# An attention and dense kernel whose instruction order comes from a planner: changed load times, engines for weight casts, and places for the q and k transposes

## The chip, the core and the metric

The kernel runs on one core of one Trainium2 chip. The core has five engines with an instruction queue each: TensorE (PE in the profile; its weight loads are shown as PEld), VectorE (DVE), ScalarE (ACT), GpSimd (POOL) and SyncE (SP), which here starts all DMA transfers. Each engine takes its instructions in the order in which the program gives them; between engines there are semaphores. The metric is the device time of one execution in microseconds. The numbers of a profile come from one profiled execution.

## What is computed

The input is q, k and v of 8 batches x 8 heads x 576 tokens x 64 channels in float32, and two weight matrices of 512 x 2048 and 2048 x 512. Cut to what matters, the reference is

```python
# attention, per batch and head
q_d, k_d, v_d = means of q, k, v over 4 tokens each      # 144 tokens
out_up    = repeat(softmax(q_d k_d^T / 8) v_d, 4)
out_local = softmax(q k^T / 8 where |i - j| < 4) v       # a band of 7
x = (out_up + out_local) as 4608 tokens x 512 channels
# dense part
h = x @ w_in                                             # 4608 x 2048
out = (h - tanh(h)) @ w_out                              # 4608 x 512
```

## The kernel before

**Attention.** Two heads of one batch make a pair: 32 pairs p, four to a batch. Two pairs make a group: 16 groups n. For a group, `load_qk(n)` brings q and k (four transfers of 288 KB) into a staging buffer `qkn`, `reorder(n, i)` casts them to bfloat16 into `qr` (i = 0 is q, i = 1 is k), and `turn(n, i)` transposes them with nine TensorE matmuls into a PSUM bank, copies the bank to `qk` and forms the sums over four tokens in two steps (`half`, then `qkd`). `qr`, `qk` and `qkd` have two buffers, one for even and one for odd groups; `half` has one. `load_v(p)` brings the v windows of a pair into one of six buffers `vst`, and `prep_v(p)` casts them to `vw`. The sums of v come from TensorE for groups 0 to 6 (`pool_v`), and from GpSimd (`load_v4`, `sum_v`, one buffer) from group 7 on.

`attention(p)` is a generator in steps: the scores of the band (`s1`, line 508, and the last tile with the pooled scores, `s2`, lines 508 and 527), three exponentials on ScalarE (lines 547, 562, 565), two multiplications with the mask on VectorE (551, 569; pairs 0 to 3 have a bias on TensorE instead, line 502), the products with v (`outs`, 580 and 586), the reciprocal `r` (595) and the scaled result `ln` (597) on VectorE. Up to pair 11 `ln` is transposed back on TensorE (631 to 635), copied (`od`, 638) and added into `xT` (640); from pair 12 on a DMA transpose does it (605) and VectorE adds (616). The scores use the banks `ps_ts`, the products with v `ps_ox`, and pairs 0 and 2 a second pair of banks, which later becomes the four banks `ps_hy` of the dense part.

**Dense part.** It has nine blocks of 512 tokens. `mm1(kb, fc)` multiplies `xT` with `w_in_sb` (line 663, four matmuls), ScalarE takes the tanh (672) and VectorE subtracts into `gT` (675). `mm2(kb, i)` multiplies `gT` with `w_out_sb` (691), ScalarE copies (702) and SyncE stores (705). From block 2 on, `mm1` of a block alternates with `mm2` of the one before. A block straddles two batches in most cases, and block 7 reaches into the last batch.

**Weights.** `load_w` brings a quarter of `w_in` or `w_out` (1 MB) in float32 into memory that is not yet in use (`gT`, late parts of `xT`), and four casts (line 397) write the bfloat16 weights. Each of them may go to one of the engines in `CAST`.

**The order.** No order is written out by hand. Every step is an `op` with an engine, a cost in nanoseconds, the buffers that it reads and writes, and a priority `pri`; `P.choice` is an op with several engines to choose from, each with a cost. `Program.order` is a list scheduler: it keeps a time at which each engine is free and each op is ready, and gives an engine that comes free the ready op with the lowest `pri`. The dense matmuls have pri 5000, so in the plan they fill what attention leaves. An op is ready when its inputs are written plus a lag by engine (`LAT`, 1800 ns for a DMA); for ops with a pri from 140 to 4999 `P.spare` adds 2500 ns behind a DMA and 1000 behind GpSimd. Transfers have planned costs: `T_QK` 760, `T_V` 800, `T_W` 2750 ns. The plan is made when the program is built; on the chip only its order remains. `idle` and `emit` find gaps of TensorE in the plan ahead of the first dense matmul, and `filler` puts matmuls on a constant there (line 869).

Where a group is reordered and turned is set in the main loop over p by program order (buffers make later readers and writers wait) and by pri (`20 * n - 12` and `20 * n`). The lists of the loop are

```python
inner = INNER.get(p, [p % 2] if p >= 2 * NP else [])    # ahead of pair p's last step
outer = OUTER.get(p, [])                                # behind it
```

so from pair 8 on, an even pair turns q of the next group and an odd pair its k. `load_qk`, `load_v` and `load_v4` of group n wait in SyncE's queue for the DMA transpose of pair 2n - 5.

Of the kernel before, what the change touches and what calls it, by code (L numbers as in the profile page):

```python
# [9 lines left out]
BF16 = mybir.dt.bfloat16  # L10
# [5 lines left out]
class Program:  # L16
# [10 lines left out]
    def __init__(self):  # L27
        self.ops = []
        self.alternatives = {}
        self.touch = []  # L30
        self.fresh = set()
        self.spare = (5000, {})
        self.last_write = {}
        self.readers = {}
# [27 lines left out]
    def order(self):  # L62
        n = len(self.ops)
# [15 lines left out]
        for _ in range(n):  # L79
# [11 lines left out]
            now, eng, i = best  # L91
# [9 lines left out]
            for u in users[i]:  # L101
                same = self.ops[u][0] == eng and eng != "DMA"
                lag = self.LAT[eng]
                if self.spare[0] <= self.ops[u][4] < 5000:
                    lag += self.spare[1].get(eng, 0)
                at[u] = max(at[u], end if same else end + lag)
                left[u] -= 1
                if left[u] == 0:
                    make_ready(u)
# [45 lines left out]
def kernel(  # L155
# [9 lines left out]
    nc = tc.nc  # L165
# [8 lines left out]
    A6 = 9  # L174
# [67 lines left out]
    P = Program()  # L242
    P.spare = (140, {"DMA": 2500, "POOL": 1000})
    op = P.op
# [50 lines left out]
    def load(ns, fn, keys, cost, pri, after=()):  # L295
        op("SP", ns, fn, reads=after, writes=list(keys) + ["queue", ("q", keys[0])],
           pri=pri)
        op("DMA", cost, None, reads=[("q", keys[0])], writes=keys, pri=pri)

    def slot_qk(n):  # L300
        return n % 2 if n >= GV else n % NQKN
# [30 lines left out]
    def load_qk(n):  # L332

        b, h0, s = n // 2, 4 * (n % 2), slot_qk(n)
        for i, src in enumerate((q, k)):
            for y in range(2):
# [7 lines left out]
                def issue(to=to, rows=rows):  # L344
                    nc.sync.dma_start(out=to, in_=rows)  # L345
                load(650, issue, [("qkn", s, i, y)], T_QK, -30,
                     [("fl", 2 * n - AHEAD)])

    def load_v(p):

        b, j, s = p // NP, p % NP, p % NVST
        t = vst[s]
# [24 lines left out]
    def load_w(src, dst, name, f, stage, keys):  # L377

        def issue():
# [4 lines left out]
            else:  # L384
# [4 lines left out]
                else:  # L389
                    nc.sync.dma_start(  # L390
                        out=stage.rearrange("p (c f) -> p c f", c=4),
                        in_=rows[:, 4 * f:4 * f + 4, :])
        load(600, issue, keys, T_W, -30)
        for c in range(4):
# [7 lines left out]
    def prep_v(p):  # L402
        s, w, jj = p % NVST, (p // 2) % NVW, p % 2
        P.choice([(eng, ns, lambda fn=fn: fn(  # L404
# [5 lines left out]
    def pool_v(hb):  # L410
# [6 lines left out]
        def mm():  # L417
# [7 lines left out]
           writes=[key], pri=pri)  # L425
        op("ACT", 300, lambda: A.copy(
            out=vd[w][:, :, :, 0:64],
# [18 lines left out]
    def turn(n, i):  # L446
# [5 lines left out]
        pri, cold = 20 * n, (1.5 if n < 1 else 1.0)  # L452
        b16 = ps.rearrange("p n c -> p (n c)").bitcast(BF16)[:, 0:A6 * 128]

        def tr():
            for a in range(A6):
                T.transpose(b16[:, 128 * a:128 * a + 128], qr[s][:, i, a, :], ident)  # L457
        P.fresh.add(len(P.ops))
        op("PE", 480 * cold, tr, reads=[("qr", s, i), "ident"], writes=ts, pri=pri)
        o = qk[s][:, :, KOFF * i:KOFF * i + 576]  # L460
# [249 lines left out]
    def dense(kb):  # L710
# [13 lines left out]
        for i in range(16):  # L724
            if kb < NBLK:
# [5 lines left out]
    XOUT, T_OUT, AHEAD = 12, 2000, 5  # L731
    MERGE, GV = 14, 7
    XADD = [("DVE", (800, 350), V)]
    ORDER, W_FIRST = "g0123", "0123g"
    INNER, OUTER = {4: [0], 5: [1]}, {3: [0, 1], 7: [0, 1]}
    T_QK, T_V, T_W, W_PRI, NEARLY = 760, 800, 2750, 33, NP
    CAST = [("POOL", 700, GP.tensor_copy), ("ACT", 520, A.copy)]
    CAST_V = [[("POOL", 720, GP.tensor_copy), ("ACT", 640, A.copy)],
              [("POOL", 790, GP.tensor_copy)]]
# [4 lines left out]
            [("ACT", 1125, A.copy)]]  # L744
    ADDERS = [[("DVE", 750, 440, V), ("POOL", 1190, 750, GP)],
              [("POOL", 1190, 880, GP)]]
# [89 lines left out]
    for p in range(NPAIR):  # L836
# [5 lines left out]
        if p >= 2:  # L842
            next(work[p])
        inner = INNER.get(p, [p % 2] if p >= 2 * NP else [])
        outer = OUTER.get(p, [])
        for i in inner if n + 1 < NGRP else []:
            reorder(n + 1, i)
            turn(n + 1, i)
        next(work[p], None)
        for i in outer:  # L850
            reorder(n + 1, i)
            turn(n + 1, i)
        if p % 2 == 1:
# [47 lines left out]
```

The softmax here doesn't subtract the row's maximum and nothing guards it: scores larger than these inputs give would overflow.

## Time and profile before

| | |
|---|---|
| median of 6 runs | 344.28 us (343.4 to 345.75) |
| profiled execution, its time | 343.4 us |
| its span in the profile | 341.7 us |
| mean granted TensorE clock | 0.985 |
| dense matmuls, L663 and L691 | 576 + 576, 292.9 us busy |
| largest on ScalarE | tanh, L672, 83.6 us in 144 |
| largest on VectorE | subtraction, L675, 95.6 us in 144 |
| largest on GpSimd | first half sum, L473, 34.3 us in 29 |
| DMA | 57.51 MB, mean 168 GB/s |

The page has six parts: busy time by engine; the span in 40 slices of 8.5 us, with a digit for the tenths busy; the DMA queues; the chain of waits that ended last; the costliest groups of instructions with the idle time of the engine before them and what ended it; and the DMA issues. Matmuls are pipelined, and the duration of one includes its way through the array, so that the time from one start to the next is the better measure of what it costs. In a timeline a row is: start, duration, engine, line, operation, operands, number of instructions, and in brackets the idle time of the engine before the row and its releaser. In a table of stages a row is: stretch and length, then busy time (instructions) of PE, PEld, DVE, ACT and POOL, then granted TensorE clock, DMA share and GB/s.

The chain that ended last runs over TensorE for 82% of the span, over DMA for 7% and over VectorE for 5%. The first dense matmul starts at 26.30 us, the last ends at 337.95.

### The profile page before, as it was taken

To read this page: it belongs to the slowest core of one execution; us is meant where nothing else is said; L and a number is where in the kernel's file an instruction comes from. 1 tells how busy PE (TensorE), PEld (TensorE's weight loads), DVE (VectorE), ACT (ScalarE), POOL (GpSimd) and SP (SyncE) were. 2 spreads that over 40 slices of the span, in tenths; PEclk is the share of its full clock that TensorE was granted. 3 is DMA by queue.
4 is the path that set the end of the run, shared out by engine and by line. 5 is a ranking of instruction groups with operands and counts; after the bars stand their busy time and mean duration, and the time that the engine had idled before them with its cause. 6 is when DMAs were issued, how large, how long until landed. Compare 5 with 4: busy or idle time off the path is not lost.

```text
span 341.7 us, 6832 instructions
## 1 busy us (share of the span) xinstructions
PE 325.2 (95%) x2616; PEld 168.4 (49%) x2616; DVE 216.1 (63%) x360; ACT 204.7 (60%) x342; POOL 151.0 (44%) x179
## 2 busy tenths in 40 slices
PE   5887999989999999999999999999999999999995
PEld 1563554645655555555555555554544444444442
DVE  4775785459987677777797668776776453343300
ACT  2685996559868665766576657665755244344411
POOL 8444847596694165939393818491300000000000
PEclk9698999999999999999999999999999999999999
DMA  6999999999802598689979579952222200100021
GB/s 209 263 389 295 280 361 322 267 296 290 220 2 59 155 248 215 187 210 193 238 162 245 157 197 214 237 155 58 59 58 60 58 31 33 61 31 33 31 88 66
DMA packets 84749, 57.51 MB, mean 168 GB/s; under 512 B 62638, under 2 KB 67822, under 8 KB 84718
## 3 DMA queue, kind: packets, MB, share of 16 engines
q1 hardware_dynamic: 84718, 57.09, 60.1%
q8 instruction: 20, 0.33, 0.4%
q14 instruction: 11, 0.09, 0.1%
HBM read 43.05 MB, written 9.44 MB: 154 GB/s over the span
## 4 chain that ended last, share of the span: by engine, by line
PE 82%; DMA 7%; DVE 5%; SPq 2%; ACT 1%; issue 1%; POOL 0%; DVEq 0%; ACTq 0%; POOLq 0%
PE ps_hy L663 34%; PE ps_hy L691 33%; PE ps_ts L457 3%; DMA vst<-in_v_dram 3%; PE ps_ts L508 3%; PE ps_ox L580 3%; DMA qkn<-in_q_dram 3%; PE ps_ox L586 2%; DVE ln L597 1%; DMA qkn<-in_k_dram 1%; SPq L369 1%; SPq L345 1%; DVE gT L675 1%; DVE qr L441 1%; PE ps_ox L457 1%
## 5 line engine op out<-in xcount | busy, mean ns | idle before, releaser
L663 PE MATMUL ps_hy<-xT,w_in_sb 128*128 128x512 bf16 x576 | 147.3, 382 | 3.4 <-DVE xT L640 2.7
L691 PE MATMUL ps_hy<-w_out_sb,gT 128*128 128x512 bf16 x576 | 145.6, 379 | 0.0
L672 ACT ACTIVATE uy<-ps_hy 128x512 f32<-128x512 f32 x144 | 83.6, 600 | 78.4 <-PE ps_hy L663 77.7
L675 DVE TENSOR_TENSOR gT<-ps_hy,uy 128x512 bf16<-128x512 f32 x144 | 95.6, 684 | 55.1 <-ACT uy L672 54.5
L663 PEld LDWEIGHTS <-w_in_sb 128*128 128x128 bf16 x576 | 53.7, 98 | 62.7 <-issue 5.9
L691 PEld LDWEIGHTS <-gT 128*128 128x128 bf16 x576 | 53.5, 98 | 59.5
L473 POOL TENSOR_TENSOR half<-qk 128x576 f32<-128x576 bf16 x29 | 34.3, 1182 | 58.3 <-ACT qk L463 57.2
L463 ACT COPY qk<-ps_ts 128x1152 bf16<-128x1152 bf16 x28 | 31.5, 1126 | 15.9 <-PE ps_ts L457 13.8
L702 ACT COPY uy<-ps_hy 128x512 f32<-128x512 f32 x36 | 21.2, 588 | 22.1 <-PE ps_hy L691 20.5
L547 ACT ACTIVATE E<-ps_ts 128x960 bf16<-128x960 f32 x30 | 29.2, 974 | 6.8 <-PE ps_ts L508 6.7
L597 DVE TENSOR_TENSOR ln<-ps_ox,r 128x896 bf16<-128x896 f32 x30 | 32.7, 1090 | 0.9
L551 DVE TENSOR_TENSOR E<-E,mask 128x960 bf16<-128x960 bf16 x28 | 22.2, 791 | 10.8 <-ACT E L547 10.5
L404 POOL CAST vw<-vst 128x640 bf16<-128x640 f32 x31 | 23.6, 774 | 10.7 <-DMA vst<-in_v_dram 8.4
L457 PEld LDWEIGHTS <-qr 128*128 128x128 bf16 x288 | 19.5, 102 | 12.6 <-DVE qr L441 5.7
L322 POOL TENSOR_TENSOR qkn<-qkn 128x512 f32<-128x512 f32 (+1 forms) x18 | 23.8, 1320 | 2.9 <-DMA qkn<-in_v_dram 2.1
L441 DVE CAST qr<-qkn 128x1152 bf16<-128x1152 f32 x18 | 15.3, 848 | 13.7 <-DMA qkn<-in_q_dram 10.6
L457 PE MATMUL ps_ts<-ident,qr 128*128 128x128 bf16 x252 | 19.1, 222 | 4.1 <-DVE qr L441 2.6
L478 POOL TENSOR_TENSOR qkd<-half 128x288 bf16<-128x288 f32 x30 | 21.7, 724 | 2.3 <-DVE half L473 1.3
L616 DVE TENSOR_TENSOR xT<-lnT 128x480 bf16<-128x480 bf16 (+1 forms) x40 | 22.0, 562 | 0.0
L441 POOL CAST qr<-qkn 128x1152 bf16<-128x1152 f32 x14 | 17.0, 1217 | 9.5 <-DMA qkn<-in_k_dram 7.7
L595 DVE RECIPROCAL r<-ps_ox 128x14 f32<-128x14 f32 x30 | 7.3, 243 | 20.0 <-PE ps_ox L586 18.1
L580 PE MATMUL ps_ox<-vw,E 128*128 128x65 bf16 x300 | 18.3, 194 | 1.2 <-DVE E L569 1.2
(87 smaller groups left out, 253.0 us busy)
## 6 DMA issues: line engine op xcount, KB each, us to landing
vst<-in_v_dram SPq DMA_DIRECT2D x62, 160.0 KB, 5.2
qkn<-in_q_dram SPq DMA_DIRECT2D x32, 288.0 KB, 3.4
qkn<-in_k_dram SPq DMA_DIRECT2D x32, 288.0 KB, 5.1
out_dram<-uy SPq DMA_DIRECT2D x36, 256.0 KB, 2.1
qkn<-in_v_dram SPq DMA_DIRECT2D x9, 512.0 KB, 4.9
gT<-in_moe_w_in_dram SPq DMA_DIRECT2D x4, 1024.0 KB, 10.1
xT<-in_moe_w_out_dram SPq DMA_DIRECT2D x8, 256.0 KB, 4.4
gT<-in_moe_w_out_dram SPq DMA_DIRECT2D x2, 1024.0 KB, 9.6
```

The costliest lines, as they stand in the source:

```text
L322: op("POOL", 1330, lambda t=t: GP.tensor_tensor(out=t[:, :, 0:2], in0=t[:, :, 0:2], in1=t[:, :, 2:4], op=ALU.add), writes=keys, pri=pri)
L441: P.choice([(eng, ns, lambda fn=fn: fn(out=dst, in_=srt)) for eng, ns, fn in REORDER[n >= 2][i]], reads=[("qkn", sn, i, x) for x in range(2)],
L457: T.transpose(b16[:, 128 * a:128 * a + 128], qr[s][:, i, a, :], ident)
L463: fn(out=o.rearrange("p y (g a) -> p y g a", a=A6), in_=b16.rearrange("p (a g y) -> p y g a", a=A6, y=2))
L473: eng.tensor_tensor(out=half, in0=four[:, :, :, 0:2], in1=four[:, :, :, 2:4], op=ALU.add)
L547: op("ACT", 980, lambda: A.activation(out=e1, in_=ps[:, :, 0:480], func=AF.Exp, scale=SCALE), reads=ts, writes=[("E", se, 0)], pri=pri)
L580: T.matmul(po[:, hh, 65 * t:65 * t + 65], E[se][:, c:c + 128], vw[w][:, 2 * jj + hh, t, :], start=True, stop=True)
L597: op("DVE", 1090, lambda: V.tensor_tensor(out=ln[sl].rearrange("p n (h d) -> p h n d", d=D), in0=blocks[:, :, :, 0:64], in1=r[s].unsqueeze ...
L663: T.matmul(ps_hy[slot], w_in_sb[:, dc, fc * 128:(fc + 1) * 128], xT[dc][:, kb * 512:kb * 512 + 512], start=(dc == 0), stop=(dc == N_DC - 1))
L672: op("ACT", 490, lambda: A.activation(out=u[us], in_=ps_hy[slot], func=AF.Tanh), reads=[("hy", slot)], writes=[("u", us)], pri=-1)
L675: op("DVE", 620, lambda: V.tensor_tensor(out=gT[g][:, fc, :], in0=ps_hy[slot], in1=u[us], op=ALU.subtract), reads=[("hy", slot), ("u", us) ...
L691: T.matmul(ps_hy[slot], gT[g][:, fc, ts * 128:ts * 128 + 128], w_out_sb[:, fc, :], start=(fc == 0), stop=(fc == N_FF - 1))
```

## The change

Nothing is computed otherwise. The change gives the planner other numbers and other program places, and the order on every engine comes out anew.

- `P.spare` becomes a function: behind a DMA 2500 ns from pri 140 on as before, and 1500 for pri 80 to 139, where there was nothing; behind GpSimd as before.
- Planned transfer costs: q and k 840 in place of 760, the k of group 0 1260; the first and second quarter of `w_in` 300 and 1400 more.
- The casts of the weights may go to VectorE too (planned at 400 ns). Planned costs on ScalarE and GpSimd change: weight casts, v casts, the copy of the pooled v (300 to 600), the half sums.
- `EARLY = 12`: up to pair 11 the lists are as before. Pair 12 turns q and k of group 7. From then on an odd pair p turns, behind its last step, q of the group after next (m = n + 2), and an even pair turns k of the next group.
- A branch of `turn` for groups from `FI` on transposes q and k by DMA into a `vst` buffer, and `slot_v` leaves two buffers free for it. `FI` is 99, there are 16 groups and 32 pairs.

```diff
-    P.spare = (140, {"DMA": 2500, "POOL": 1000})
+    def spare(pri, eng):
+        if eng == "DMA":
+            return 2500 if pri >= 140 else 1500 if pri >= 80 else 0
+        return 1000 if eng == "POOL" and pri >= 140 else 0
+    P.spare = spare
...
+    def slot_v(p):
+        return p % 4 if p >= 2 * FI else p % NVST
...
-                load(650, issue, [("qkn", s, i, y)], T_QK, -30,
+                load(650, issue, [("qkn", s, i, y)],
+                     T_QK + (500 if n == 0 and i == 1 else 80), -30,
                      [("fl", 2 * n - AHEAD)])
...
-        load(600, issue, keys, T_W, -30)
+        load(600, issue, keys, T_W + (W_LATE[f] if src is moe_w_in else 0), -30)
...
-        op("ACT", 300, lambda: A.copy(
+        op("ACT", 600, lambda: A.copy(
...
+        if n >= FI:
...
-        P.fresh.add(len(P.ops))
-        op("PE", 480 * cold, tr, reads=[("qr", s, i), "ident"], writes=ts, pri=pri)
+        if n < FI:
+            P.fresh.add(len(P.ops))
+            op("PE", 480 * cold, tr, reads=[("qr", s, i), "ident"], writes=ts, pri=pri)
...
+    FI, T_IN, EARLY = 99, 2600, 12
...
+    W_LATE = [300, 1400, 0, 0]
...
-    CAST = [("POOL", 700, GP.tensor_copy), ("ACT", 520, A.copy)]
-    CAST_V = [[("POOL", 720, GP.tensor_copy), ("ACT", 640, A.copy)],
+    CAST = [("POOL", 620, GP.tensor_copy), ("ACT", 620, A.copy),
+            ("DVE", 400, V.tensor_copy)]
+    CAST_V = [[("POOL", 790, GP.tensor_copy), ("ACT", 720, A.copy)],
...
-    ADDERS = [[("DVE", 750, 440, V), ("POOL", 1190, 750, GP)],
+    ADDERS = [[("DVE", 760, 440, V), ("POOL", 1190, 850, GP)],
...
-        inner = INNER.get(p, [p % 2] if p >= 2 * NP else [])
-        outer = OUTER.get(p, [])
+        inner = INNER.get(p, [] if p < 2 * NP else [p % 2] if p < EARLY else
+                          [0, 1] if p == EARLY else [1] if p % 2 == 0 else [])
+        m = n + 1 + (p > EARLY)
+        outer = OUTER.get(p, [0] if p > EARLY and p % 2 else [])
...
-        for i in outer:
-            reorder(n + 1, i)
-            turn(n + 1, i)
+        for i in outer if m < NGRP else []:
+            reorder(m, i)
+            turn(m, i)
```

The number and kind of instructions stay, but for seven more filler matmuls (10 become 17). Of the eight weight casts that go to VectorE, five are of `w_in`. The SyncE queue keeps the order of its loads.

## The prediction, made before the changed kernel was run

> **What bounds the kernel now.** I read the page's shares first, then the slices, then TensorE's timeline with its idle times, then the same stretches on VectorE and ScalarE, then busy times by stage.
>
> ```profile
> PE 325.2 (95%) x2616; PEld 168.4 (49%) x2616; DVE 216.1 (63%) x360; ACT 204.7 (60%) x342; POOL 151.0 (44%) x179
> ...
> PE   5887999989999999999999999999999999999995
> ...
> DMA  6999999999802598689979579952222200100021
> ```
>
> TensorE is the bound: 325.2 of 341.7 us. The 1152 dense matmuls stay, and in long runs they start every 0.216 us (8 in 1.73 us in the chain of waits), so they are 248.8 us that no order shortens. What an order can save is TensorE's idle time and slow clock. The idle time lies at the start, where DMA is full, and in four places later:
>
> ```profile
> 29.32 3.18 PE L663 MATMUL ps_hy<-xT,w_in_sb 128*128 128x512 bf16 x8 [1.20 <-DVE xT L640]
> 57.51 0.23 PE L631 MATMUL ps_ox<-ident,ln 128*128 128x128 bf16 x1 [0.61 <-DVE ln L597]
> 69.10 0.38 PE L508 MATMUL ps_ts<-qk 64*128 64x120 bf16 x8 [1.01 <-ACT qk L463]
> 77.19 0.20 PE L580 MATMUL ps_ox<-vw,E 128*128 128x65 bf16 x1 [1.22 <-DVE E L569]
> 273.20 3.46 PE L663 MATMUL ps_hy<-xT,w_in_sb 128*128 128x512 bf16 x14 [0.67 <-ACT uy L702]
> ```
>
> In brackets is the idle time before a row and who ended it: 0.61 + 1.01 + 1.22 = 2.84 us in the middle. At the end 0.67 understates it: the 8 matmuls that started at 270.63 should have handed over at 272.36, so 0.84 is lost, and the 14 take 3.46 where 14 x 0.216 and the last one's tail of 0.16 make 3.19, 0.27 more: 1.1 us. From 77 to 270 us nothing else stands still. Behind the middle stalls stands one pattern:
>
> ```profile
> 55.16 1.01 DVE L441 CAST qr<-qkn 128x1152 bf16<-128x1152 f32 x1 [2.35 <-DMA qkn<-in_q_dram]
> ...
> 68.04 1.12 DVE L441 CAST qr<-qkn 128x1152 bf16<-128x1152 f32 x1 [1.35 <-DMA qkn<-in_q_dram]
> ...
> 76.20 0.76 DVE L441 CAST qr<-qkn 128x1152 bf16<-128x1152 f32 x1 [3.37 <-DMA qkn<-in_q_dram]
> ```
>
> VectorE takes its instructions in order. The planner believed these q loads to be in earlier, and put the casts of groups 4, 6 and 7 ahead of work that TensorE waits for: r and ln of pair 5, ln of pair 7, the second mask (L569) of pair 8.
>
> **Middle stalls.** I compared the issue orders of the two kernels. In the new one the cast of group 4 stands behind ln of pair 5 and the first mask of pair 6, that of group 6 behind ln of pair 7, that of group 7 behind ln of pair 8. So the masks of pair 8 now stand behind group 6, which landed at 68.0, and no longer behind group 7, which landed at 76.2. That takes 0.61 and 1.22 away. The 1.01 at 69.10 is another chain: ScalarE's copy of group 4's k waited 2.02 us for GpSimd's half sum of q, which ran at 66.73 behind a cast that waited for group 5's k (63.84), a memset (0.95) and a v cast (0.73). In the new order the half sum stands ahead of all but the v casts that landed by 59.6. q is turned after 104 dense matmuls, not 110 (6 x 0.216 = 1.3 us earlier, about 61.8); its copy (1.12) ends about 63.5, the half sum (1.15) at 64.7, the copy of k at 66.0, and S1 of pair 8 falls due at about 66.8. Nothing is waited for. What is late next is group 7's q (76.2): behind it stand a subtraction and the mask of pair 9, due near 77, so the cover is thin; I keep 0.3 for it. Sum: -2.84 + 0.3 = -2.5.
>
> **End stall.** q of group g was turned in pair 2g-2 and k in pair 2g-1. From group 8 on, q is turned as pair 2g-3 ends, and k in pair 2g-2. The attention of the next group no longer waits for transpose, copy (1.12), half sum (1.18) and sum (0.72) of k within its last pair, so the planner packs pairs closer: from pair 12 to pair 31 there were 31 dense matmuls a pair (216 to 810), and there are 24 (230 to 680). Block 7 of the dense part, which starts at dense matmul 832, needs pair 31. Before, that was 22 matmuls behind; the planner split block 7 (2, then 8 of the second product, then 14) and the banks ran out at 273.2. Now pair 31 is 152 matmuls (33 us) ahead, and the order there is the even 8 and 8 seen later without a gap. -1.1.
>
> **Start.** The loads and their order are the same, so the landings are too. Three q/k casts go from VectorE to GpSimd (0.76 or 1.58 becomes about 1.15), two q/k copies from ScalarE to VectorE (1.12 becomes 1.36), one v cast from ScalarE to GpSimd, and five w_in casts come to VectorE. I follow the path to xT of pair 3, which starts the dense stream. k of group 0 is cast at 7.98 + 1.2 = 9.2, where VectorE was ready at 9.56. Its transpose, copy and sums then run as before within 0.3 us; q of group 1 is about 0.3 later, and the v copies (vd) follow both last exponentials of pair 1, which shifts outs of pair 0 from 17.8 to about 18.4-18.9. ln of pair 0 ends at 20.4 (was 19.98). The VectorE queue from there: two w_in casts, xT 0.75, ln of pairs 2 and 1, a cast, two xT, ln of pair 3 (1.09), then transposes and xT. The sum of the rows puts xT of pair 3 at 29.7, where it was 29.27: +0.4. Two prices in it are open.
>
> First the casts: VectorE shows no 512-column cast. From the 1152-column row (0.76) I estimate 0.37 each; but that form took 1.58 at 7.98, while GpSimd ran a half sum. The Trainium skill (GPSIMD Engine Reference, Specifications) says that both engines share the SBUF interfaces and contend when VectorE runs a two-port mode. It speaks against this part: a slab's casts now start on both engines as it lands. With the quiet row the three casts ahead of the last ln cost 1.1, with the disturbed one 2.3. Two would run beside GpSimd's two casts (1.2 us at 19.8), so I add 0.3 of the 1.2: start +0.7.
>
> Second the clock:
>
> ```profile
> 3.90:7.30 3.40, 1.62 (x13) 0.62 (x11) 0.78 (x1) 0.71 (x1) 3.33 (x8) 1.00 0.90 291
> 7.30:10.70 3.40, 1.09 (x10) 1.09 (x11) 2.33 (x2) 0.41 (x1) 2.41 (x3) 0.61 1.01 324
> ...
> 20.90:24.30 3.40, 2.73 (x69) 2.29 (x67) 2.63 (x5) 2.70 (x8) 1.21 (x4) 1.00 1.04 386
> 24.30:27.70 3.40, 1.47 (x12) 0.75 (x13) 3.19 (x5) 2.09 (x5) 1.74 (x4) 1.00 1.06 391
> 27.70:31.10 3.40, 2.20 (x12) 0.97 (x11) 1.22 (x2) 1.91 (x4) 1.18 (x2) 0.63 1.11 342
> ```
>
> The first figure after the length is TensorE's busy time, the third from the right its granted clock. The skill (TensorE: Matmul & The Clock Gate, What's actually happening) lets the clock fall to half after at least one idle window of about 3.4 us; by that, no gap here (1.5 us at most) costs clock, and the seven filler matmuls that are added gain nothing. The rows disagree: behind windows busy 1.62 and 1.47 of 3.40 the clock fell (0.61, 0.63), behind 2.73 it held. The new fillers (five for two) make the window from 3.9 about 1.95 busy. If that holds the clock, transposes and scores from 9 to 14 us run twice as fast and the path gains 0.9; if not, nothing. 1.95 is nearer to 1.62 than to 2.73, so I take nothing; -0.9 stays for the range.
>
> **The faster stretch.** A pair took (262.5 - 97.8)/19 = 8.7 us. With 24 for 31 dense matmuls it is 1.5 us shorter, 7.2. Per pair VectorE has ln 1.09, r 0.24, masks 0.79 + 0.47, xT 0.79 + 0.33, half a q cast 0.42 and three subtractions of 0.68: 6.2 of 7.2 (86%). The cover is there: from 80 to 100 us it was busy 18.7 of 20 and TensorE had no gap. GpSimd has 5.4 of 7.2, ScalarE about the same. DMA stood at 0.81 from 140 to 220; times 8.7/7.2 that is 0.98, full. A group's loads took 12.5 us from the first q to the pooled v4, of 14.4 that a group now lasts, and q is wanted about 13 us after its trigger. It fits without much room: +0.4 for small waits. TensorE's turns into 64-row scores (0.31 for 0.22 to the next start) grow by about three, +0.3 at most, within that.
>
> **Sum.** -2.5 - 1.1 + 0.7 + 0.4 = -2.5. The profiled execution took 343.4 (span 341.7, 1.7 around it), so 340.9 against it. It is also the fastest of the six shown, whose median is 0.9 above; I forecast the median of the new one at **341.8**.
>
> **Rivals.**
> - *The stalls move instead of going* (0.20). DMA is full to 77 us, and no load lands sooner; TensorE, with 1-2 us fewer dense matmuls done, would meet the next cast at 76.2. For it: no landing moves. Against it: the masks no longer stand behind that cast. Then only the end goes: 343.4 - 1.1 + 0.7 + 0.4 = 343.4; median 344.3, no change.
> - *Slower: the fuller loads hold up the pooled sums* (0.15). From group 9 on GpSimd puts all four v4 sums (4.3 us) between q's two sums, and k's follow. If v4 lands over 2 us later than 12.5 us after its q, GpSimd waits, k's sums slip by as much, and beyond some 5 us of slack TensorE waits at S1 of each next group. It decides from 0.5 us a group (seven groups, 3.5 us). At 1 us: 340.9 + 7 = 347.9; median 348.8. For it: DMA at 0.98. Against it: two margins, together 7 us.
> - *The start gains as well* (0.10, faster): clock held and quiet casts, -0.9 and -0.3: 340.6.
> - The branch with the DMA transpose never runs (FI = 99) and `slot_v` gives the old slot: that part does nothing.
>
> **Numbers.** The forecast has 0.55, the rivals 0.20, 0.15 and 0.10. A difference under 0.3% (1.0 us) can't be told from none. Faster: 0.55 + 0.10, plus 0.03 of the first rival: 0.68. Same: 0.15. Slower: 0.15 and 0.02 of the first: 0.17. Range 339.5 (all stalls gone, clock held, no new waits) to 345.2, which takes in the first rival and leaves out most of the second.
>
> **What would show it.** Right: no idle time over 0.3 us on TensorE from 50 to 100 us, none near 273, block 7 in even runs, VectorE near 86% until about 240 us and GpSimd done by then; the first 8 dense matmuls at 29.5-30.2. Wrong: waits of L508 for qkd or qk from 120 us on (second rival), L569 again behind a load, or a dense stream that starts past 31.

## The result, and the profile after

The changed kernel took 347.81 us in the median of 29 runs (343.81 to 351.72), the kernel before 344.82 us of 66 (343.04 to 348.88). The ratio is 1.0058 [1.0041, 1.0076]: **slower by 0.6%**, where 341.8 and "faster" were forecast, and outside the range of 339.5 to 345.2. All ratios here leave out the slow runs, those over 1.5% above the fastest of their kernel (11 of the changed kernel's 30 with the profiled one), which is why this one is below the quotient of the two medians, 1.0087. The profiled execution (351.08 us) is one of the longest of its kernel, for a reason given under the clock below.

The page of the changed kernel, in the lines that were shown of before, and the chain of work that ended last (shares of the span by engine):

```profile
PE 329.4 (94%) x2623; PEld 168.4 (48%) x2623; DVE 238.2 (68%) x369; ACT 200.9 (57%) x334; POOL 159.1 (46%) x178
...
PE   5777999999999999999999999999999999999995
...
DMA  6999999999900599796979959552200100010021
...
PE 63%; DVE 24%; DMA 4%; ACT 3%; issue 2%; SPq 2%; ACTq 0%; DVEq 0%
```

The same line of the page before:

```profile
PE 82%; DMA 7%; DVE 5%; SPq 2%; ACT 1%; issue 1%; POOL 0%; DVEq 0%; ACTq 0%; POOLq 0%
```

VectorE works 22 us longer on nearly the same list, and its share of the chain goes from 5% to 24%. TensorE's timeline after (start, length, instruction, idle time ahead of it), at the places that the prediction named:

```profile
31.23 5.13 PE L682 MATMUL ps_hy<-xT,w_in_sb 128*128 128x512 bf16 x13 [1.20 <-DVE xT L659]
...
62.74 0.72 PE L428 MATMUL ps_ox<-vw,pick 128*128 128x256 bf16 x5 [0.71 <-DVE xT L659]
...
85.40 0.20 PE L599 MATMUL ps_ox<-vw,E 128*128 128x65 bf16 x1 [0.43 <-DVE E L588]
...
99.18 0.59 PE L682 MATMUL ps_hy<-xT,w_in_sb 128*128 128x512 bf16 x2 [0.73 <-DVE gT L694]
...
270.36 1.89 PE L682 MATMUL ps_hy<-xT,w_in_sb 128*128 128x512 bf16 x8
272.08 1.03 PE L710 MATMUL ps_hy<-w_out_sb,gT 128*128 128x512 bf16 x4
```

The stalls of before at 57, 69, 77 and 273 us are gone; three shorter ones have come between 60 and 100 us. The dense stream, counted from its first unbroken row, starts at 31.23 us, past the 31 that the prediction had named as a sign of being wrong; in a second profile of the same kernel (a_again) it starts at 29.88. (Line numbers have moved: L441 of before is L450 now, L457 is L475, L508 is L527, L551 and L569 are L570 and L588, L580 is L599.) The loss sits where before there was no gap at all. Busy times by stage, before and then after (PE, PEld, DVE, ACT, POOL, then clock, DMA share, GB/s):

```profile
140.00:180.00 40.00, 40.00 (x343) 21.09 (x341) 31.38 (x51) 26.36 (x44) 27.69 (x28) 1.00 0.81 192
180.00:220.00 40.00, 40.00 (x337) 20.77 (x336) 29.01 (x50) 25.78 (x43) 22.46 (x24) 1.00 0.81 211
```

```profile
140.00:180.00 40.00, 38.10 (x362) 20.14 (x361) 35.23 (x53) 26.78 (x42) 31.05 (x31) 1.00 0.85 215
180.00:220.00 40.00, 37.87 (x351) 19.85 (x350) 36.45 (x53) 26.37 (x42) 29.89 (x30) 1.00 0.93 224
```

VectorE goes from 60.4 to 71.7 of 80 us, TensorE loses its unbroken row. A scene out of these 80 us (timeline of the changed kernel, engines mixed):

```profile
197.81 1.17 POOL L450 CAST qr<-qkn 128x1152 bf16<-128x1152 f32 x1
197.90 1.69 DVE L450 CAST qr<-qkn 128x1152 bf16<-128x1152 f32 x1
...
199.65 0.68 PE L475 MATMUL ps_ts<-ident,qr 128*128 128x128 bf16 x9 [0.70 <-DVE qr L450]
...
201.62 1.15 POOL L492 TENSOR_TENSOR half<-qk 128x576 f32<-128x576 bf16 x1 [1.45 <-ACT qk L482]
201.80 1.08 DVE L588 TENSOR_TENSOR E<-E,mask 128x192 bf16<-128x192 bf16 x1
...
202.94 0.20 PE L599 MATMUL ps_ox<-vw,E 128*128 128x65 bf16 x1 [0.76 <-DVE E L588]
```

VectorE casts q while GpSimd casts k, begun 0.09 us earlier: 1.69 us for what took 0.76 before. TensorE's turn of q waits 0.70 for it. At 201.80 the small mask starts 0.18 behind GpSimd's half sum and ends 0.11 behind its end, after 1.08 us, and TensorE waits 0.76 in the middle of `outs`.

**A measure for all runs.** TensorE's *lost time* up to a moment is that moment less the sum, over the matmuls begun by then (fillers left out), of what each takes from start to start in an unbroken run. Records of dense matmuls that were missing in a trace are put in at the gap they leave. Each figure of lost time is from one profiled execution. The last two columns are the ratio, formed as above, and the quotient of the medians over all runs of the kernel and of the kernel before beside it.

| kernel | to 40 us | 40-100 | 100-end | of it 140-220 | time / before | medians |
|---|---|---|---|---|---|---|
| before, two profiles | 17.9; 19.4 | 5.3; 6.7 | 11.5; 11.9 | 5.0; 4.9 | 1 | 1 |
| changed, two profiles | 20.6; 18.8 | 5.4; 4.1 | 16.4; 16.2 | 11.8; 10.3 | 1.0058; 1.0055 | 1.0087; 1.0066 |
| a_lists_old | 20.1 | 3.8 | 11.7 | 5.1 | 0.9926 | 0.9933 |
| b_lists_new | 18.0 | 7.0 | 12.8 | 7.5 | 1.0040 | 1.0027 |
| a_no_dve_cast | 16.5 | 6.0 | 18.4 | 11.1 | 1.0116 | 1.0107 |
| a_loads_only | 17.0 | 4.1 | 12.9 | 6.1 | 0.9969 | 0.9975 |
| a_no_sumv | 18.7 | 2.7 | 15.1 | 9.9 | 0.9979 | 0.9986 |
| a_half_sub | 17.4 | 3.2 | 14.0 | 8.4 | 1.0001 | 1.0036 |
| a_k_act | 16.6 | 3.5 | 14.2 | 8.6 | 0.9989 | 1.0024 |
| a_q_first | 20.1 | 5.1 | 13.6 | 8.9 | 1.0007 | 1.0039 |
| a_early_20 | 19.9 | 4.9 | 14.2 | 7.1 | 0.9975 | 1.0001 |
| a_true_costs | 19.2 | 6.3 | 19.2 | 7.5 | 1.0171 | 1.0191 |
| a_old_fill, twice | 16.3; 17.2 | 4.0; 3.5 | 11.0; 10.7 | 5.0; 5.0 | 0.9884; 0.9919 | 0.9908; 0.9900 |
| a_loads_fill | 17.9 | 4.3 | 13.7 | 6.1 | 1.0027 | 1.0038 |
| b_fill | 17.6 | 5.7 | 11.6 | 5.0 | 0.9981 | 0.9988 |
| a_new_fill_k | 17.7 | 3.7 | 13.3 | 8.6 | 0.9957 | 0.9962 |
| a_old_fill_k | 19.4 | 4.3 | 12.2 | 5.6 | 0.9948 | 0.9940 |

Before against changed, by the means of two profiles: +1.0 to 40 us, -1.3 from 40 to 100, +4.6 from 100 on. The sum of 4.3 is that of these four executions, whose times differ by 4.1; the medians of all runs differ by 3.0.

The start varies more between executions than between the kernels. Eight profiles have the changed kernel's order up to 40 us (changed, a_lists_old, a_no_sumv, a_half_sub, a_k_act, a_q_first, a_early_20): they lost 16.6 to 20.6 there, 19.0 in the mean. Three have the order of before (before, b_lists_new): 17.9 to 19.4, 18.4 in the mean.

### The profile page after: what moved, and what is told of

The parts are those of the page before. It is cut to its first block, busy times and chain, and to the rows that moved or that the text cites. A ratio compares the mean times of both kernels' runs of the same rounds, so it can differ in the third digit from the quotient of the medians.

```text
span 349.3 us, 6853 instructions
## 1 busy us (share of the span) xinstructions
PE 329.4 (94%) x2623; PEld 168.4 (48%) x2623; DVE 238.2 (68%) x369; ACT 200.9 (57%) x334; POOL 159.1 (46%) x178
## 4 chain that ended last, share of the span: by engine, by line
PE 63%; DVE 24%; DMA 4%; ACT 3%; issue 2%; SPq 2%; ACTq 0%; DVEq 0%
PE ps_hy L710 28%; PE ps_hy L682 25%; DVE gT L694 7%; DVE E L570 4%; DVE xT L635 3%; DVE qr L450 3%; DVE ln L616 3%; PE ps_ts L475 2%; DVE E L588 2%; DMA gT<-in_moe_w_in_dram 2%; PE ps_ox L599 2%; PE ps_ts L527 2%; SPq L378 2%; PE ps_ox L605 1%; DMA qkn<-in_k_dram 1%
## 5 line engine op out<-in xcount | busy, mean ns | idle before, releaser
L492 POOL TENSOR_TENSOR half<-qk 128x576 f32<-128x576 bf16 x28 | 33.0, 1179 | 38.1 <-ACT qk L482 24.4
L482 ACT COPY qk<-ps_ts 128x1152 bf16<-128x1152 bf16 x26 | 29.2, 1124 | 13.8 <-PE ps_ts L475 12.8
L566 ACT ACTIVATE E<-ps_ts 128x960 bf16<-128x960 f32 x30 | 29.0, 971 | 11.2 <-PE ps_ts L527 11.1
L721 ACT COPY uy<-ps_hy 128x512 f32<-128x512 f32 x36 | 21.1, 587 | 17.8 <-PE ps_hy L710 17.7
L413 POOL CAST vw<-vst 128x640 bf16<-128x640 f32 x32 | 28.9, 910 | 4.2 <-PE ps_ox L599 1.8
L570 DVE TENSOR_TENSOR E<-E,mask 128x960 bf16<-128x960 bf16 x28 | 25.9, 926 | 5.1 <-ACT E L566 5.0
L450 POOL CAST qr<-qkn 128x1152 bf16<-128x1152 f32 x17 | 21.0, 1238 | 12.3 <-DMA qkn<-in_k_dram 11.6
L635 DVE TENSOR_TENSOR xT<-lnT 128x480 bf16<-128x480 bf16 (+1 forms) x40 | 25.7, 663 | 0.0
L475 PEld LDWEIGHTS <-qr 128*128 128x128 bf16 x288 | 17.8, 98 | 14.6 <-DVE qr L450 7.9
L330 POOL TENSOR_TENSOR qkn<-qkn 128x512 f32<-128x512 f32 (+1 forms) x18 | 23.7, 1319 | 0.7
L475 PE MATMUL ps_ts<-ident,qr 128*128 128x128 bf16 x252 | 18.7, 219 | 4.3 <-DVE qr L450 4.3
L599 PE MATMUL ps_ox<-vw,E 128*128 128x65 bf16 x300 | 19.4, 194 | 2.6 <-DVE E L588 2.5
L599 PEld LDWEIGHTS <-E 128*128 128x128 bf16 x300 | 15.7, 98 | 10.5 <-DVE E L588 3.5
L450 DVE CAST qr<-qkn 128x1152 bf16<-128x1152 f32 x15 | 18.5, 1235 | 2.2 <-DMA qkn<-in_q_dram 2.2
```

The lines of the kernel that those rows point to most:

```text
L450: P.choice([(eng, ns, lambda fn=fn: fn(out=dst, in_=srt)) for eng, ns, fn in REORDER[n >= 2][i]], reads=[("qkn", sn, i, x) for x in range(2)],
L482: fn(out=o.rearrange("p y (g a) -> p y g a", a=A6), in_=b16.rearrange("p (a g y) -> p y g a", a=A6, y=2))
L492: eng.tensor_tensor(out=half, in0=four[:, :, :, 0:2], in1=four[:, :, :, 2:4], op=ALU.add)
L570: op("DVE", 700, lambda: V.tensor_tensor(out=e1, in0=e1, in1=mask[:, 0:480].unsqueeze(1).to_broadcast([128, 2, 480]), op=ALU.mult), reads= ...
L599: T.matmul(po[:, hh, 65 * t:65 * t + 65], E[se][:, c:c + 128], vw[w][:, 2 * jj + hh, t, :], start=True, stop=True)
L635: up=up: eng.tensor_tensor(out=xo[:, QW * t0:QW * t0 + nt * n].rearrange("p (t g a) -> p t g a", t=nt, a=4), in0=lnT[sl][:, t0:t0 + nt, 0: ...
```

## Experiments

**The parts taken apart.** Two theories stood at first: V, that the new lists pack the pairs closer than VectorE can follow; S, that the loss lies at the start, with VectorE's weight casts. First the changed kernel once more, and with the old lists:

> The changed kernel once more, beside the three others. Both theories: about 0.6% over the kernel before. Theory V (VectorE is the bound in the faster stretch): TensorE again loses 5 to 7 us between 140 and 220 us, in waits for masks (L588) and q casts (L450) on VectorE. Theory S (the start): xT of pair 3 is again near 31.2 us instead of 29.3 and the clock is at half for two windows behind it; in runs with full clock the time should then be below 344.

> The changed kernel with the lists of before (EARLY = 99: q in the even pair, k in the odd pair of the group ahead); weight casts on VectorE and the new planned loads stay. Pairs are at 30 dense matmuls again (pair 31 at 794). Theory V: the waits from 140 to 220 us go, middle stalls stay away, the start keeps its cost: 343 to 345. Theory S: little changes, 346 to 347.

```diff
-    FI, T_IN, EARLY = 99, 2600, 12
+    FI, T_IN, EARLY = 99, 2600, 99
```

The repeat gave 1.0055 [1.0024, 1.0086]; from 140 to 220 us TensorE lost 5.3 us more than before, and two runs with full clock took 345.3 and 345.6 us, where S had them below 344. With the old lists the same kernel is *faster* than before, 0.9926 [0.9893, 0.9959]; from 140 to 220 us it loses 5.1 us, like before. TensorE's waits from 100 to 280 us (us in total, times, longest), in the changed kernel and then with the old lists:

```profile
PE ps_ox L599 <- DVE E L588: 2.1, 4, 0.8
PE ps_ts L475 <- DVE qr L450: 1.8, 3, 0.7
PE ps_ox L428 <- DVE xT L659: 0.2, 1, 0.2
```

```profile
PE ps_ox L599 <- DVE E L588: 0.4, 1, 0.4
PE ps_ox L428 <- DVE xT L659: 0.3, 1, 0.3
```

Then the lists alone, in the kernel before, and the change without VectorE's weight casts:

> The kernel before with the new lists alone (EARLY = 12); no weight casts on VectorE, old planned loads. Pairs are at 25 dense matmuls (pair 31 at 698). Theory V: the middle stalls stay, the end stall goes, and VectorE makes TensorE wait 4 to 7 us from 140 to 220: 347 to 350. Theory S: 343 to 344, the end stall saved.

> The changed kernel without VectorE among the engines for weight casts; lists and planned loads are the new ones (pair 31 at 680). Theory V: the stretch keeps its waits, the start gains 1 to 2: 345 to 346.5. Theory S: 342 to 344, xT of pair 3 near 29.5.

```diff
-            ("DVE", 400, V.tensor_copy)]
```

The lists alone cost 1.0040 [1.0022, 1.0059]. That is a loss, but less than V forecast: from 140 to 220 us TensorE lost 2.5 us more than before, not 4 to 7. The windows of this run:

```profile
140.00:180.00 40.00, 39.95 (x374) 21.65 (x372) 34.16 (x55) 28.82 (x47) 32.03 (x32) 1.00 1.04 224
180.00:220.00 40.00, 39.44 (x359) 20.74 (x358) 35.96 (x54) 26.50 (x43) 32.76 (x32) 1.00 0.93 224
```

VectorE is busy for 70.1 of 80 us, nearly as in the changed kernel (71.7), its pairs are as close (7.18 us), and the small mask is as long (0.58); but q's cast takes 0.78 us there where the changed kernel has 1.29, and TensorE stands idle for 0.6 us where it has 4.0. A full VectorE alone is not what costs most.

Without VectorE's weight casts the changed kernel was slower still, 1.0116 [1.0071, 1.0161]: S falls, and V's 345 to 346.5 us were missed too. The loss lies from 100 us on (18.4); other planned times gave another order, and which part of it costs this is not shown. That the casts cost at the start isn't shown either: 16.5 us were lost there without them and 17.0 in a_loads_only, but 16.6 in a_k_act, which has them.

**Why VectorE, and how.** Four ways to relieve it with the new lists in place:

> The changed kernel with GpSimd's two-step sums of v (L330, L336, about 4.3 us a group) not issued from group 7 on, everything else in the same planned order. It leaves out the pooled values of v of those groups. Theory V1 (VectorE is the bound from 140 to 220 us, and it is so because its bf16 operations stand still beside GpSimd's): q cast from 1.44 to under 1.1 us, second mask from 0.58 to under 0.45, VectorE's 71.3 of 80 us falls to 66 or less, TensorE's loss from 100 to 280 us falls from 16.1 to about 12.5, time about 344.5 (1.0% under the changed kernel). Theory V2 (VectorE has too much work by itself, contention or not): its rows stay within 10%, the loss stays above 15, time within 0.3% of the changed kernel. Theory Q (GpSimd's own queue is late): time falls as well, but VectorE's rows keep their length.

```diff
-            op("POOL", 1330, lambda t=t: GP.tensor_tensor(
-                out=t[:, :, 0:2], in0=t[:, :, 0:2], in1=t[:, :, 2:4], op=ALU.add),
+            op("POOL", 1330, lambda: None,
...
-                    GP.tensor_tensor(out=vd[w][pp, i, :, 0:64], in0=t[:, :, 0],
-                                     in1=t[:, :, 1], op=ALU.add)
+                return None
```

0.9979 [0.9953, 1.0005], 0.75% under the changed kernel. VectorE's rows shortened with nothing changed on VectorE: q cast 1.44 to 1.23, second mask 0.58 to 0.36 (100 to 230 us), its work from 140 to 220 us 71.3 to 66.1. So GpSimd's work does lengthen VectorE's rows. But q's cast stayed over the 1.1 that V1 asked for, and from 100 us on only 1.1 of the 4.6 came back, where V1 had 3.6; the rest of the gain lies between 40 and 100 us. V1 holds for most of the rows and for part of the time.

> The changed kernel with the dense subtraction on VectorE (L694) cut to 256 of its 512 columns from dense block 2 on (from about 92 us). It leaves out half of each gT tile of those blocks; the planned order is the same, and the instructions that TensorE was seen to wait for (q cast, both masks) are untouched. It takes about 0.3 us x 3 per pair from VectorE. Theory V (VectorE as a whole is the bound from 140 to 220 us): TensorE's loss from 100 to 280 us falls from 16.1 to 13 or less, time about 345 (0.8% under the changed kernel). Theory O (only the place of single instructions in VectorE's queue, as the mask behind the q cast): loss stays above 15, time within 0.3% of the changed kernel.

```diff
+        w = 512 if kb < 2 else 256
-            out=gT[g][:, fc, :], in0=ps_hy[slot], in1=u[us], op=ALU.subtract),
+            out=gT[g][:, fc, 0:w], in0=ps_hy[slot][:, 0:w], in1=u[us][:, 0:w],
+            op=ALU.subtract),
```

1.0001 [0.9974, 1.0027], loss from 100 us on 14.0: between the two theories. Work that TensorE was never late for, taken off VectorE, gave back 2.2 us: the load on VectorE counts too. (q's cast, untouched, took 1.15 us here, since the two casts met at other moments; so the 2.2 aren't the subtraction's alone.)

> The changed kernel in its planned order, with the casts of k from group 8 on issued on ScalarE in place of GpSimd, at the same place in the order. Theory M (the stalls of 130 to 220 us come from q's cast on VectorE running beside k's cast on GpSimd, which makes it 1.69 us instead of 0.76): q cast falls from 1.44 to about 0.9 us, TensorE no longer waits for qr, its loss from 100 to 280 us falls from 16.1 to 14 or less, time 1.5 to 3 us under the changed kernel (0.997 to 1.001 of before). Theory D (closeness of the pairs as such, many small waits): q cast shorter, but loss above 15 and time within 1 us of the changed kernel; ScalarE's later exponentials could even make it slower.

```diff
-        P.choice([(eng, ns, lambda fn=fn: fn(out=dst, in_=srt))
+        P.choice([(eng, ns, lambda fn=A.copy if i and n > GV else fn: fn(out=dst, in_=srt))
```

> The changed kernel with q's cast from group 7 on taken by VectorE as soon as the planner believes its data in (priority 33 earlier). Pair 31 is planned at dense matmul 698 for 680. Theory M: q's cast then runs ahead of k's, takes about 0.8 us, the turn of q no longer waits, loss from 100 to 280 us 14 or less. Theory B (the pattern of the kernel before: a cast put ahead of masks waits for its load and holds them up): the waits of TensorE go over to the masks, loss 16 or more.

```diff
-                 writes=[("qr", s, i)], pri=20 * n - 12)
+                 writes=[("qr", s, i)], pri=20 * n - (45 if i == 0 and n >= 7 else 12))
```

With k's cast on ScalarE: 0.9989 [0.9962, 1.0016], loss 14.2 (M had 14 or less). With q's cast first: 1.0007 [0.9975, 1.0039], loss 13.6. Both speak for M: 2 to 2.7 us of the 4.6 came back. But in a_q_first the two casts still run at the same time in six of the seven groups from 100 to 230 us; what changed is which starts first, now q's in four of the six. One group there:

```profile
151.48 0.75 DVE L450 CAST qr<-qkn 128x1152 bf16<-128x1152 f32 x1
151.53 1.70 POOL L450 CAST qr<-qkn 128x1152 bf16<-128x1152 f32 x1 [0.21 <-DMA qkn<-in_k_dram]
```

q's cast starts 0.05 us ahead and keeps its 0.75; now it is k's that takes 1.70. Over the profiles with the new lists the loss from 140 to 220 us goes with the length of q's cast: 10.3 to 11.8 us at 1.29 to 1.44, 8.4 to 9.9 at 1.15 to 1.23, 7.5 to 8.9 at 0.78 to 0.92. With the old lists and in the kernel before it is 5 to 6. The row of q's cast in a_k_act from 100 to 230 us, and the waits that are left to TensorE there until 280 us:

```profile
L450 DVE CAST qr<-qkn 128x1152 bf16<-128x1152 f32 x7 | 6.2, 893 | 0.0
```

```profile
PE ps_hy L682 <- ACT uy L721: 1.3, 3, 0.6
PE ps_ox L599 <- DVE E L588: 0.6, 1, 0.6
```

q's cast is at 0.89, and TensorE no longer waits for it. ScalarE's own copies (L721) are late instead.

> The changed kernel, new lists and all, with the durations that the trace shows given to the planner for VectorE: masks 900 and 580 for 700 and 220, q cast 1440 for 860, sums of x 770 and 610 for 800 and 350, the dense subtraction 690 for 620. The planner then puts pair 31 at dense matmul 812 instead of 680. Theory V (the lists let the planner pack pairs closer than VectorE can do them, because VectorE's prices are too low): the loss of TensorE from 100 to 280 us falls from 16.1 to 12 or less, time 343 to 344, as with the old lists. Theory L (the new lists themselves are bad, by where q and k are turned): stays within 1 us of the changed kernel, 347 to 348.

```diff
-            op("DVE", 700, lambda: V.tensor_tensor(
+            op("DVE", 900, lambda: V.tensor_tensor(
...
-            op("DVE", 220, lambda: V.tensor_tensor(
+            op("DVE", 580, lambda: V.tensor_tensor(
```

(The q cast, the sums of x and the subtraction likewise.) A clear miss of V: 1.0171 [1.0127, 1.0216]. The spread-out pairs did take the loss of 140 to 220 us to 7.5, but the new order has gaps of other kinds: 1.7 us for pooled k at 74 us, the end stall of before again (0.84 at 282 us; pair 31 at 812), and two windows at half clock behind such gaps. Truer prices gave no better plan.

> The changed kernel with the new lists from pair 20 on instead of pair 12; pair 31 is then planned at dense matmul 746, between 680 (changed) and 794 (old lists). Theory V: pairs 12 to 20 keep the old distance, the new stalls come only behind pair 20, so the time lies between the old lists (0.9926 of before) and the changed kernel (1.0055): 0.997 to 1.001. If closeness of the pairs is harmless and the step at pair 12 itself does the harm (the place where q and k are both turned in one pair), the step is as dear at pair 20: 1.003 or more.

```diff
-    FI, T_IN, EARLY = 99, 2600, 12
+    FI, T_IN, EARLY = 99, 2600, 20
```

0.9975 [0.9950, 1.0000], with 7.1 us lost from 140 to 220 us: between old and new lists, as V forecast.

**The middle, the start and the clock.**

> The changed kernel with the old lists and without VectorE among the engines for weight casts: what is left of the change is the planned time of the first loads and the other prices. With the old lists and VectorE's casts it was 0.9926 of before. Theory P (the gain is that of the planned loads, which take the middle stalls away): 0.992 to 0.995 of before, and idle time of TensorE under 0.6 us at each place from 50 to 90 us. Theory C (weight casts on VectorE carry the gain): 0.998 to 1.003, within 0.3% of before.

> The kernel before, unchanged, profiled once more, since its first profile is of the fastest of its six runs. Expected: the same stalls at about 57, 69, 77 and 273 us; a loss of TensorE from 100 to 280 us of 11 to 12 us; and 1 to 2 us more at the start, where the clock falls a second time or for longer.

a_loads_only is the `EARLY = 99` of a_lists_old without VectorE's line in `CAST`. It took 0.9969 [0.9944, 0.9994], between P and C, and two waits of 0.8 and 0.9 us were left where P had none over 0.6. The middle loses 4.1 us there, and 7.0 with the lists alone, which speaks for the planned time of the loads and the prices as what mends the middle. Which of the two, no run tells apart; and a_no_dve_cast, with both, lost 6.0. b_again (346.85 us in its one run) shows the stalls of before once more, and what a long one costs. Its timeline (TensorE) and its windows (TensorE's busy time behind the length, its clock third from the right):

```profile
78.95 0.20 PE L580 MATMUL ps_ox<-vw,E 128*128 128x65 bf16 x1 [1.73 <-DVE E L569]
...
79.39 4.01 PE L663 MATMUL ps_hy<-xT,w_in_sb 128*128 128x512 bf16 x10
```

```profile
75.90:79.30 3.40, 1.67 (x27) 0.91 (x26) 1.34 (x3) 1.71 (x4) 1.45 (x3) 1.00 0.96 290
79.30:82.70 3.40, 3.40 (x17) 1.22 (x14) 3.21 (x6) 2.31 (x4) 0.72 (x1) 0.52 0.77 161
```

The stall left TensorE busy for 1.67 of 3.40 us, and the next 3.4 us ran at half clock: ten dense matmuls took 4.01 us. The changed kernel has this at the start of the dense part:

```profile
7.30:10.70 3.40, 2.99 (x20) 1.12 (x17) 3.27 (x4) 0.00 (x0) 1.91 (x2) 1.00 1.03 337
...
24.30:27.70 3.40, 2.54 (x33) 2.11 (x34) 3.04 (x6) 1.56 (x4) 1.85 (x4) 0.66 1.05 388
27.70:31.10 3.40, 2.06 (x10) 0.85 (x9) 2.08 (x4) 1.44 (x4) 1.12 (x2) 0.50 1.07 368
31.10:34.50 3.40, 3.27 (x8) 1.13 (x8) 2.77 (x5) 1.19 (x2) 1.55 (x2) 0.50 1.02 197
```

With the seven fillers the clock held from 7.3 us on (0.61 before), but nothing came of it: 13.6 us lost by 20 us, against 13.0 and 12.3. (In a_early_20, with the same fillers, it fell at 7.9 us all the same.) From 25 to 35 us the clock fell for three windows. So I put 12 more fillers there (theory K):

> The changed kernel with the old lists (0.9926 of before) and 12 more filler matmuls ahead of the places where TensorE waits from 22 to 30 us. Theory K (the clock falls to half for 3.41 us behind a window of 3.41 us in which TensorE was busy less than about half, seen behind windows busy 1.68 us or less and never behind 1.70 or more; the start of the dense part then runs at half speed for one to three windows): no window at half speed between 24 and 36 us, the loss of TensorE at 40 us falls from 20.1 to 18 or less, time 1 to 2 us under 343.3, say 0.988 of before. Theory D (the start waits for loads, and the clock there costs nothing): loss at 40 us stays within 0.7 of 20.1, time within 0.3% of the old lists.

> The same 12 fillers in the kernel with the old lists and without VectorE's weight casts (0.9969 of before; its profile had a full clock from 14 us on by itself, and its runs spread from 342.1 to 348.4). Theory K: the profile looks the same as without, but the spread of the runs shrinks and the median falls by 1 to 2 us, to 0.991 to 0.994 of before. Theory D: 0.995 to 0.999, spread unchanged.

> The kernel before with the same 12 fillers from 22 to 30 us. Its two profiles had one and two windows at half speed from 28 us on. Theory K (the clock at the start of the dense part costs time): no half window between 24 and 36 us, median 1 us or more under before (0.997 or less). Theory D (it costs nothing, or fillers delay the work by as much): 0.999 to 1.004.

```diff
+            fill.update(self.extra)
...
+        if p in (2, 3):
+            P.extra[i] = ("ox1", 5) if p == 2 else ("ox", 2)
...
+            if kb == fc == 0 and part == 1:
+                P.extra[i] = ("ox", 5)
```

Here `i` is the transpose back (L650 to L654) of that pair, or the first dense matmul that needs pair 3. With the old lists: 0.9884 [0.9845, 0.9923], 16.3 us lost by 40 us for 20.1: a hit of K. Without VectorE's casts 1.0027 [1.0004, 1.0050], a miss: that profile had kept its clock from 14 us on without fillers, 17.9 us were lost at the start for 17.0, and more from 100 us on (13.7 for 12.9); why, isn't shown. In the kernel before 0.9981 [0.9963, 0.9999], a gain, but short of K's 0.997. In all profiles with the 12 fillers no window from 22 to 36 us ran at half clock, as in a_old_fill2 (below); in 11 of the 14 others one to three did.

**Put together.**

> The changed kernel (new lists) with both cures: the 12 fillers from 22 to 30 us, and the casts of k from group 8 on issued on ScalarE. Theory M+K (the meeting of the casts and the clock at the start are all that is wrong with the change): as good as or better than the old lists with the same two edits, 0.988 to 0.992 of before. Theory D (the closeness of the pairs costs 1.5 to 2 us by itself): 0.993 to 0.997, and slower than its twin with the old lists by 0.4 to 0.6%.

> The old lists with fillers, and the casts of k from group 8 on issued on ScalarE. In the kernel with the old lists q's cast took 0.99 us (0.76 alone), and TensorE never waited for it: 0.988 to 0.990 of before, no gain over the same kernel without the move, if M is right that only a waited-for cast is worth moving; 0.984 or less if GpSimd's share of memory slows TensorE's path everywhere.

> The old lists with fillers once more, unchanged, on the chip of the two others. 0.986 to 0.991 of before if the first six runs stand for it; 0.992 to 0.994, like the old lists without fillers, if they were lucky.

New lists with both cures 0.9957 [0.9936, 0.9978]: what theory D forecast, so the meeting of the casts and the clock aren't all that is wrong with the change. Old lists with both 0.9948 [0.9925, 0.9971], for 0.988 to 0.990 forecast; old lists with fillers alone 0.9919 [0.9897, 0.9940] again, at the edge between the two forecasts. Moving k's cast off GpSimd brought nothing there, where TensorE had not waited for q's. Cured, the new lists beat before, but not the old lists with fillers. a_old_fill beats both kernels: 341.77 and 341.95 us in its medians of six runs each. How much of that the fillers give stays open: the old lists without them had 0.9926, measured beside other runs, and the intervals overlap; by 40 us the four profiles with this start and the fillers lost 16.3 to 19.4 us, the eight without 16.6 to 20.6. Its windows in the second profile:

```profile
24.30:27.70 3.40, 2.55 (x34) 1.44 (x31) 3.18 (x6) 1.70 (x4) 1.31 (x3) 1.00 1.07 392
27.70:31.10 3.40, 3.28 (x21) 1.57 (x20) 2.20 (x5) 2.03 (x4) 0.62 (x1) 1.00 1.09 346
31.10:34.50 3.40, 3.40 (x27) 1.87 (x26) 2.53 (x5) 2.77 (x5) 2.29 (x3) 1.00 0.98 212
```

## Why the prediction was wrong

- **The faster stretch (+0.4): the step that failed.** From 100 us on TensorE lost 4.6 us more, though the end stall of 1.1 had gone: the closer pairs cost about 5.7, for 0.4 forecast. Their distance was told right: 7.21 us over pairs 14 to 30 for the 7.2 forecast (8.61 before). VectorE's work per pair was mis-sized, 6.2 us for what came to nearly 7, because the rows were those of the looser schedule and contention with GpSimd was put at nothing there. Before and after, from 100 to 230 us:

```profile
L551 DVE TENSOR_TENSOR E<-E,mask 128x960 bf16<-128x960 bf16 x16 | 13.2, 823 | 7.0 <-ACT E L547 6.8
L569 DVE TENSOR_TENSOR E<-E,mask 128x192 bf16<-128x192 bf16 x16 | 7.5, 468 | 0.4 <-ACT E L562 0.4
L441 DVE CAST qr<-qkn 128x1152 bf16<-128x1152 f32 x7 | 5.5, 780 | 0.0
```

```profile
L616 DVE TENSOR_TENSOR ln<-ps_ox,r 128x896 bf16<-128x896 f32 x18 | 19.6, 1088 | 0.5
L570 DVE TENSOR_TENSOR E<-E,mask 128x960 bf16<-128x960 bf16 x18 | 16.9, 941 | 4.3 <-ACT E L566 4.3
...
L588 DVE TENSOR_TENSOR E<-E,mask 128x192 bf16<-128x192 bf16 x18 | 9.9, 552 | 1.9 <-ACT E L581 1.9
...
L450 DVE CAST qr<-qkn 128x1152 bf16<-128x1152 f32 x7 | 9.0, 1290 | 0.0
```

  With these, and 0.82 and 0.61 for the sums of x, the sum of the forecast is 6.95 us a pair and not 6.2: 96% of 7.21 (from 140 to 220 us the profile has VectorE busy for 90%). But b_lists_new is as full and as close and loses, with its end stall gone too, only about 2.2 us to it. Another 2 to 2.7 us came back when q's cast no longer started behind k's; about 1 us is left over. The cover I cited (18.7 of 20 us from 80 to 100) was a stretch at the old distance. I weighed the contention with GpSimd for two casts at the start (0.3 us), and left it out of the stretch where GpSimd became busier too.
- **The middle stalls (-2.5): half of it or more.** All three went, but by the lost time only 1.3 came in (two profiles each), since shorter stalls stand in their place (three in the first profile, two in the second). With a_half_sub and a_k_act, which change nothing before 90 us and lost 3.2 and 3.5 here, it is 2.0. The loads' planned time as the cause has support (4.1 us lost in a_loads_only, 7.0 in b_lists_new), but no run changes it alone.
- **The end stall (-1.1): right**, and by its reason. With pair 31 at 810 or 812 dense matmuls the gap is there (before, a_true_costs), at 794 or earlier it is gone; so the old lists with the new loads lose it too, and the new lists aren't needed for it.
- **The start (+0.7): not refuted, and not shown.** The eight profiles with this start lost 0.6 more in the mean than the three of before, with a spread of 4 us for one and the same order. The sign named against it, a dense stream past 31 us, showed in one of the eight; the others have 28.99 to 30.29. The rival "the start gains as well" had its cause happen, a held clock from 7 to 14 us, without the gain.
- **The rivals.** The one on the slower side, v4 late at GpSimd, did not occur: its sums (L330) waited 0.7 us in the whole run, and the DMA share was 0.85 and 0.93 where 0.98 was forecast. That its verdict, "slower", came true is no merit of its reason. I had looked for the danger in loads and not in the engine at 86%.
- What stays open: b_lists_new loses only 1.1 us more from 100 us on than before, the changed kernel 4.6. The meeting of the two casts explains 2 to 2.7 of the difference of 3.5, if what a_k_act and a_q_first gave back is all theirs (ScalarE and the order of other steps changed with them). For the rest only "another order" can be said.

## What to carry to other kernels

A row's mean belongs to the density at which it was measured: before an engine is planned to 86%, ask what else runs beside it and which of the two starts first, and take its rows from the moments when both run. Compare orders in stretches, by lost time, and try each part of a change alone; here a gain of 0.7% hid behind a loss of 1.3%. A planner that decides greedily by prices gives another order for every price, so a better price is not yet a better plan.

## What the runs showed of the hardware

**VectorE beside GpSimd.** From both profiles of the changed kernel, behind the first 40 us, mean us of instructions with GpSimd idle (under 5% of their time) and working (over 80%): q cast 0.75 (a single one) and 1.35, large mask 0.65 and 1.04, small mask 0.25 and 0.84, small sum of x 0.25 and 0.78. What reads PSUM stays as it is: ln 1.09 and 1.09, the dense subtraction 0.69 and 0.68, the reciprocal 0.24 and 0.24.

The means hide that it goes by who starts first. In all 20 profiles, behind 40 us, 69 of VectorE's casts of q or k overlap one on GpSimd. In 31 VectorE's starts first, or within 0.03 us of GpSimd's: it takes 0.74 to 0.76 us in 27 of them, and GpSimd's 1.17 to 1.78. In the 38 others GpSimd's starts earlier, by 0.05 us or more: VectorE's takes 0.82 to 1.71, 21 times 1.69 or more, and GpSimd's 1.14 to 1.62.

**The clock goes by half-busy windows.** The traces give it in pieces of 3.41 us. Over 20 profiles it fell from full to half 20 times inside the kernels, 19 times behind a window with TensorE busy for 1.68 us or less, once at 1.94; the windows behind which it held, about 1850, had 1.58 us or more. From half it rose behind 2.62 us or more, and stayed behind 2.59 or less but for one at 2.84. The 30 runs of the changed kernel fall into groups by the number of windows at half, as their mean clock gives it: median 346.2, 347.7, 349.3 and 350.5 us for none, one, two and three, about 1.4 us each. Most of the spread of its runs goes with this. It is no rule for every kernel: in the 22 runs of b_fill none, one and two such windows go with 344.4, 344.3 and 344.2 us. Its profile has them from 8 to 15 us, while the changed kernel's lie at the start of the dense part.
